# First attention batch: squares, narrowing steps and one subtraction in other places of the order, and unread products ahead of some waits

## The chip, the cores and the metric

One core of a Trainium2 chip. The metric is the device time of one execution in microseconds (us); several executions are run and the median is given. The engines are TensorE (PE; its weight loads are a row of their own, PEld), VectorE (DVE), ScalarE (ACT), GpSimd (POOL) and SyncE (SP), which only issues DMAs here.

## The reference

Three stages, all in float32. Attention over 4 batches, 12 heads, 448 positions and 64 channels, with q and k normalized by their root mean square:

```
q_n, k_n = rmsnorm(q, g_q), rmsnorm(k, g_k)        # x / sqrt(mean(x*x) + 1e-6) * g
scores = 1/sqrt(64) * q_n @ k_n.T ; scores -= max(scores, axis=-1)
attn = exp(scores) ; attn /= sum(attn, axis=-1) + 1e-9
x = attn @ v                                       # to [1792, 768]
h = x @ w_in ; g = h * clip(h + 3, 0, 6) / 6 ; x = g @ w_out      # 768 -> 2048 -> 768
```

Then a mixture of 8 experts with a fixed capacity of 224 tokens each: the gate's logits are sorted, every token gets an expert that still has room, and each expert applies a two-layer net with a relu. w_in and w_out arrive with 64 bits per element and have to be narrowed to float32 first.

## The kernel before, in words

**Units of work.** Attention runs over 24 pairs of heads, six to a batch: pair i is batch i // 6, and both heads of a pair are worked on together, one on partitions 0 to 63, one on 64 to 127. The dense layer 1 of a batch (`mlp1_atoms`, 16 units of 18 matmuls) can start when all six pairs of it are done, so the first batch of attention runs without it. From batch 1 on, matmuls of the dense layer of the batch before are dealt out between those of attention.

**What a pair does**, with the names that the prediction uses. `load` (L224): q and k by DMA. `squares` (L248, ScalarE, one call for q and one for k into two buffers `sq`), `fold` (L253, GpSimd, halves them), `sums` (L259, VectorE), `guess` (L269, VectorE), `invert` (L274: three Newton steps of four instructions each, on GpSimd for pairs 1 to 9, over one pair or a group of two), `norm` (L289, GpSimd: normalized `xn` of q and k). `transp` (L310) for q and k: four TensorE transposes each, then ScalarE writes the high part (`qh`, `kh`) and VectorE the low part (`ql`, `kl`). `s1` (L333), four chunks: two score matmuls and two row maxima `mx` on VectorE. `mt` (L345): the maxima transposed by TensorE, spread by VectorE (`mr`). `sT` (L353), four chunks: eight matmuls for the transposed scores with the maxima subtracted, two exponentials on ScalarE (`ph`). `pv` (L444): 16 matmuls for the output; ScalarE copies it to `xn_t`, of which there are two buffers. `psums` (L454): matmuls with ones sum the exponentials; ScalarE writes `rb`. From pair 6 on GpSimd first adds the exponentials in twos (`padd`, L439).

**The round trip.** The sums of a pair go to DRAM (`rs_out`, L469), come back in another layout (`rs_in`, L474), VectorE takes reciprocals (`rec`, L479), these go to DRAM (`r_out`, L485) and come back broadcast (`r_in`, L490). GpSimd multiplies `xn_t` with them (`xmul`, L495); `xsplit` (L499) writes the high part `xh` of the result on ScalarE and the low part `xl` on GpSimd. The `xl` of pair i frees the buffer into which `xn_t` of pair i+2 is copied. The last pair of batch 0 (pair 5) and of the whole run take another way (`av`, `normalize`, `xt`, L376 to L434).

**Narrowing.** `conv` (L150): for each of 16 units of w_in, a DMA of 768 KB, one ScalarE step and three VectorE steps (L141 to L144), and a DMA of the narrowed 384 KB. Two buffers hold the raw units, so the load of unit u+2 waits until the last step of unit u is done.

**The order.** Nothing is scheduled by a planner: every engine issues in program order, and that order is a list of events, each with a due time written by hand (`at`, L737, and the loop from L746). A pair takes 16 units of this time, pair i is shifted by 16 i, and the list is sorted. Within a pair `squares` come at -50, `invert` at -42 (groups of two from pair 4 to 9: -35.5), `transp` of q at -30 and of k at -28, `s1` from -24, `mt` at -9, `sT` from 0, `pv` at 15.6; in batch 0 (TX0, L79) the round trip and the two parts of x at 20, 23, 27, 29, 32.5, 39, 42 and 46. Unit u of w_in is loaded 14 ahead of 20 + 10 u (T_CI and D_CI, L81), its four steps stand at +0 to +3 and its store at +5 (L792 to L796). The squares of the second pair of a group stand 4 units after the first's (L752). Since every engine is strictly in order, an instruction that has to wait holds back all that stands behind it on its engine; so does a DMA in SP's queue that waits for its data.

PSUM tiles have eight buffers under one tag; a tile's first writer waits for the reader of the buffer's tenant before.

Of the kernel before, what the change touches and what calls it, by code (L numbers as in the profile page):

```python
# [10 lines left out]
BF16 = mybir.dt.bfloat16  # L11
# [10 lines left out]
def kernel(  # L22
# [14 lines left out]
    nc = tc.nc  # L37
# [8 lines left out]
    NP = H // 2  # L46
# [24 lines left out]
    T_SUMS, T_INV, T_INV0, NG0 = -50, -42, -35.5, 10  # L71
# [4 lines left out]
    T_ADD, T_PV, T_SUM = (6, 13), (15.6, 15.62, 15.64, 15.66), 15.7  # L76
    T_RS, T_RL, T_REC, T_RO, T_RB, T_X, T_XH, T_XL = 19.5, 21.5, 24, 25.5, 28, 33, 35.5, 39.5
    GD, WD2, C_ST = 12, 8, 5
    TX0 = (20, 23, 27, 29, 32.5, 39, 42, 46)  # L79
    QMAJOR = (NP - 1, B * NP - 1)  # L80
    T_CI, D_CI, T_CO, D_CO, T_CL = 20, 10, 180, 12, 14  # L81


    order = ExitStack()
# [3 lines left out]
    const = ctx.enter_context(tc.tile_pool(name="const", bufs=1, side="left"))  # L88
# [12 lines left out]
    def load_scales():  # L101
        for s in range(2):
            for t, src in ((gq8, g_q), (gk, g_k)):
                nc.sync.dma_start(t[64 * s:64 * s + 64, :], bass.AP(tensor=src.tensor, offset=src.offset, ap=[[1, D], [1, 1]]))
        nc.vector.tensor_scalar(gq8, gq8, 1.0 / math.sqrt(D), None, op0=OP.mult)

    half = const.tile([128, 1], F32, name="half")
    nc.vector.memset(half, 0.5)
# [201 lines left out]
    def transp(i, which):  # L310

        x = QKV[i][which]
        t = ps.tile([128, 512], F32, name="t", tag="b", bufs=8)
        for c in range(NCH):
            nc.tensor.transpose(t[:, c * CP:(c + 1) * CP], x[:, c].rearrange("p h d -> p (h d)"), ident[:CP, :CP])
        g = (gq8, gk)[which]
        h = apool.tile([128, S], F32R, name="qk"[which] + "h", bufs=OB)
        l = apool.tile([128, S], F32R, name="qk"[which] + "l", bufs=OB)
        if which == 0:
            order = "d (c p) -> d p c", "d (p c) -> d p c"  # L320
            tt, ho, lo = t[:, :S].rearrange(order[0], c=NCH), h.rearrange(order[1], c=NCH), l.rearrange(order[1], c=NCH)
        else:
            tt, ho, lo = t[:, :S], h, l
        hi = nc.scalar.activation(ho, tt, AF.Copy, scale=g)
        if which == 1:
            FIRST.setdefault("ka", hi)
        nc.vector.scalar_tensor_tensor(lo, tt, g, ho.bitcast(F32), op0=OP.mult, op1=OP.subtract)
        OPER.setdefault(i, []).extend((h, l))
# [4 lines left out]
    def s1(i, c):  # L333
        qh, ql, kh, kl = OPER[i]
        MX[i] = mxs[i % 2]
        pp = [ps.tile([128, 512], F32, name="s1", tag="b", bufs=8) for _ in ROWS]
        for s, r in enumerate(ROWS):
            mm = nc.tensor.matmul(pp[s][:CP, :S], qh[r, c * CP:(c + 1) * CP], kh[r], start=True, stop=True)  # L338
            MX.setdefault("first", mm)
        for s in range(2):  # L340
            mx = nc.vector.tensor_reduce(MX[i][:, s, c:c + 1], pp[s][:CP, :S], axis=AX.X, op=OP.max)  # L341
        if c == NCH - 1:
            FIRST.setdefault("mx", mx)

    def mt(i):  # L345
        t = ps.tile([128, 512], F32, name="t", tag="b", bufs=8)
        nc.tensor.transpose(t[:, :CP], MX[i].rearrange("p h c -> p (h c)"), ident[:CP, :CP])
        MR[i] = apool.tile([128, NCH, CP], F32R, name="mr")
        nc.vector.tensor_tensor(MR[i], t[:, None, :CP].to_broadcast([128, NCH, CP]), place, op=OP.mult)
# [103 lines left out]

    def psums(i):  # L454
        p = ps.tile([128, 512], F32, name="sm", tag="b", bufs=8)
        if i < NP:
            for c in range(NCH):
                for s in range(2):
                    r = (c % 2 * 2 + s) * QW
                    nc.tensor.matmul(p[r:r + QW, :S], ones32, PP[i, s, c][0], start=(c < 2), stop=(c >= 2))  # L460
        else:
            for n in range(2):
                for s in range(2):
                    r = (2 * n + s) * QW
                    nc.tensor.matmul(p[r:r + QW, :S], ones32, PA.pop((i, s, n)), start=True, stop=True)  # L465
        RB[i] = apool.tile([128, S], F32, name="rb", bufs=2)
        nc.scalar.activation(RB[i], p[:, :S], AF.Identity, bias=heps)
# [269 lines left out]
    def at(t, fn, *args):  # L737
        events.append((t, len(events), fn, args))
# [7 lines left out]
    for i in range(NH // 2):  # L746
        t = 16 * i
        at(t + T_LOAD, load, i)
        at(t + T_VLOAD, vload, i)
        g = GROUP[i]  # L750
        first = 16 * g[0]
        t_sq = first + T_SUMS + 4 * (i - g[0])  # L752
        at(t_sq, squares, i)
        if 2 <= i < NG0:
            at(t_sq + 2, fold, i)
            t_sq += 3
        at(t_sq, sums, i)
        late_g = 4 <= g[0] < NG0
        if i == g[-1]:
            at(t_sq if 2 <= i < NG0 else first + T_INV, guess, g)  # L760
            at(first + (T_INV0 if late_g else T_INV), invert, g)
# [28 lines left out]
    at(8 * H + 2, prefetch, 0)  # L790
    at(8 * H + 14, prefetch)
    for u in range(NF if wide else 0):  # L792
        for out_, t in ((0, T_CI + D_CI * u), (1, T_CO + D_CO * u)):
            at(t - T_CL, conv, (out_, u), -1)
            for part in (0, 1, 2, 3, C_ST):
                at(t + part, conv, (out_, u), part)  # L796
# [446 lines left out]
    for pi, (t, hfs) in enumerate(passes):  # L1243
        if t not in YT:
            YT[t] = gp.tile([128, DM], F32, name="ysb", bufs=2)
        pp = {hf: ps.tile([128, 512], F32, name="y", tag="b", bufs=8) for hf in hfs}
# [7 lines left out]
        for f in range(NF):  # L1254
            i, k = divmod(f, QF)
# [139 lines left out]
```

## Time and profile before

| | us |
|---|---|
| median of 3 runs | 1164.75 |
| lowest and highest | 1159.02, 1165.14 |
| the profiled execution, its own time | 1162.06 |
| its span, first to last instruction | 1160.2 |
| TensorE, weight loads, VectorE, ScalarE, GpSimd busy | 1099.2 (95%), 880.7 (76%), 692.2 (60%), 521.3 (45%), 464.6 (40%) |
| mean granted clock of TensorE | 0.979 of full speed |

The share of busy time is an average over stages: attention with the narrowing (to about 130 us for the first batch), attention with the dense layer between (to about 500), the dense layers, the routing and the experts. Busy time of TensorE is modelled from the starts of its matmuls and can't show how fast it ran; the granted clock and the distance between matmuls do. All times in rows are from the start of the span. In a timeline row the start comes first, then the busy time, and the brackets give how long the engine stood idle before and what released it.

### The profile page before, as it was taken

How to read it: one execution, taken by the hardware profiler on the slowest of the kernel's cores; microseconds unless marked ns; L12 is line 12 of the kernel's file. 1: busy time of each engine (PE TensorE's matmuls, PEld its weight loads, DVE VectorE, ACT ScalarE, POOL GpSimd, SP SyncE). 2: the span in 40 equal slices, each digit the busy share in tenths (PEclk: the TensorE clock that was granted, in tenths of full speed). 3: DMA queues.
4: the chain of work that ended last, by engine and by line, in shares of the span. 5: the costliest groups of instructions: out<-in, count | busy, mean ns of one | idle time of the engine just before them, and what ended most of it. 6: DMA issues, size and time to landing. Idle time of an engine off the chain costs nothing.

```text
span 1160.2 us, 19232 instructions
## 1 busy us (share of the span) xinstructions
PE 1099.2 (95%) x7073; PEld 880.7 (76%) x7073; DVE 692.2 (60%) x1440; ACT 521.3 (45%) x941; POOL 464.6 (40%) x410
## 2 busy tenths in 40 slices
PE   4978899999999999999999999999997999999997
PEld 3446556766766667787767888888887899999997
DVE  7877877886677845212341666666665846555550
ACT  4655555745545556533542111111114766666551
POOL 4665555664445533112444000000004677775540
PEclk9987989999999999999999999999998999999999
DMA  4575998978777887659996222222237888877731
GB/s 133 145 197 148 248 300 252 309 238 297 251 250 253 257 288 239 222 190 276 356 310 204 78 69 82 64 76 71 70 104 185 245 262 247 248 227 217 226 130 39
DMA packets 215357, 232.17 MB, mean 200 GB/s; under 512 B 28296, under 2 KB 188384, under 8 KB 215264
## 3 DMA queue, kind: packets, MB, share of 16 engines
q1 hardware_dynamic: 211936, 219.94, 61.6%
q0 software_dynamic: 3328, 11.01, 3.1%
q8 instruction: 55, 0.90, 0.3%
q14 instruction: 38, 0.31, 0.1%
HBM read 179.82 MB, written 51.09 MB: 199 GB/s over the span
## 4 chain that ended last, share of the span: by engine, by line
PE 67%; DVE 10%; DMA 9%; issue 5%; POOL 4%; ACT 3%; SPq 1%; POOLq 0%; DVEq 0%; ACTq 0%
PE y L1195 19%; PE h L559 15%; PE y L1347 8%; PE h L1283 5%; PE st L360 4%; PE av L449 4%; PE h L1285 3%; DMA w_hl<-w 2%; DMA we_s<-in_moe_w_dram 2%; DVE mx L341 2%; PE rt L988 1%; PE lg L601 1%; PE sm L465 1%; DMA gr<-g_dr 1%; DVE cv L143 1%
## 5 line engine op out<-in xcount | busy, mean ns | idle before, releaser
L559 PE MATMUL h<-xh,w 128*128 128x448 f32 x768 | 239.9, 382 | 1.0 <-DVE mx L341 0.5
L559 PEld LDWEIGHTS h<-xh,w 128*128 128x128 f32 x768 | 143.3, 191 | 35.9 <-issue 22.1
L559 PE MATMUL h<-xl,w 128*128 128x448 f32 x384 | 145.7, 379 | 0.0
L341 DVE TENSOR_REDUCE mx<-s 112x1 f32<-112x448 f32 x192 | 105.9, 611 | 51.6 <-PE s L338 51.3
L1133 ACT ACTIVATE g2h<-gr 128x512 fp32r<-128x512 f32 x60 | 37.9, 631 | 206.1 <-PE y L1195 161.6
L1195 PE MATMUL y<-woh,g2l 128*128 128x512 f32 (+1 forms) x448 | 124.8, 344 | 1.0 <-POOL g2l L1098 1.0
L1195 PE MATMUL y<-woh,g2h 128*128 128x512 f32 (+1 forms) x448 | 125.3, 345 | 0.0
L1195 PE MATMUL y<-wol,g2h 128*128 128x512 f32 (+1 forms) x448 | 125.2, 344 | 0.0
L1098 POOL TENSOR_TENSOR g2l<-gr,g2h 128x512 fp32r<-128x512 f32 x14 | 19.0, 1361 | 240.6 <-DMA gr<-g_dr 209.0
L119 POOL TENSOR_TENSOR wel<-we_s,weh 128x768 fp32r<-128x768 f32 x48 | 96.3, 2010 | 45.4 <-ACT weh L118 37.0
L118 ACT ACTIVATE weh<-we_s 128x768 fp32r<-128x768 f32 x107 | 88.4, 841 | 57.9 <-DMA we_s<-in_moe_w_dram 39.3
L119 DVE TENSOR_TENSOR wel<-we_s,weh 128x768 fp32r<-128x768 f32 x59 | 78.3, 1334 | 60.3 <-ACT weh L118 53.6
L371 ACT ACTIVATE ph<-st 112x448 f32<-112x448 f32 x192 | 93.0, 545 | 40.8 <-PE st L360 39.7
L442 POOL TENSOR_TENSOR pa<-ph 112x448 f32<-112x448 f32 x68 | 85.6, 1279 | 44.2 <-ACT ph L371 44.2
L1283 PE MATMUL h<-xe,weh 128*128 128x448 f32 x318 | 100.4, 375 | 2.0 <-DVE xe L1234 2.0
L559 PEld LDWEIGHTS h<-xl,w 128*128 128x128 f32 x384 | 73.2, 191 | 11.9 <-issue 7.0
L1195 PEld LDWEIGHTS y<-woh,g2l 128*128 128x128 f32 x448 | 72.0, 189 | 10.7 <-POOL g2l L1098 1.3
L1195 PEld LDWEIGHTS y<-woh,g2h 128*128 128x128 f32 x448 | 71.9, 189 | 10.6 <-issue 1.5
L1195 PEld LDWEIGHTS y<-wol,g2h 128*128 128x128 f32 x448 | 71.9, 189 | 9.1 <-issue 0.7
L1285 PE MATMUL h<-xe,wel 128*128 128x224 f32 x318 | 76.6, 268 | 0.0
L562 ACT ACTIVATE r<-h,half 128x448 f32<-128x448 f32 x64 | 40.6, 634 | 77.7 <-PE h L559 67.3
L497 POOL TENSOR_TENSOR xn_t<-xn_t,rb 128x448 f32<-128x448 f32 x22 | 25.8, 1175 | 119.7 <-DMA rb<-rec_dr 119.7
(252 smaller groups left out, 2386.1 us busy)
## 6 DMA issues: line engine op xcount, KB each, us to landing
we_s<-in_moe_w_dram SPq DMA_DIRECT2D x128, 384.0 KB
w<-w_hl SPq DMA_DIRECT2D x32, 768.0 KB
gr<-g_dr SPq DMA_DIRECT2D x52, 256.0 KB
wraw<-in_moe_w_in_dram SPq DMA_DIRECT2D x16, 768.0 KB
win_v<-w SPq DMA_DIRECT2D x32, 384.0 KB
w_hl<-w SPq DMA_DIRECT2D x16, 768.0 KB
wraw<-in_moe_w_out_dram SPq DMA_DIRECT2D x16, 768.0 KB
g_dr<-g SPq DMA_DIRECT2D x48, 224.0 KB
```

The lines of the kernel that those rows point to most:

```text
L118: nc.scalar.activation(hi, raw, AF.Copy)
L119: eng.tensor_tensor(lo, raw, hi.bitcast(F32), op=OP.subtract)
L341: mx = nc.vector.tensor_reduce(MX[i][:, s, c:c + 1], pp[s][:CP, :S], axis=AX.X, op=OP.max)
L360: nc.tensor.matmul(pp[s][:CP, :S], a[r], b[r], start=(n == 0), stop=(n == len(todo) - 1))
L371: nc.scalar.activation(e, pp[s][:CP, :S], AF.Exp)
L442: nc.gpsimd.tensor_tensor(PA[i, s, n], PP[i, s, 2 * n][0], PP[i, s, 2 * n + 1][0], op=OP.add)
L449: nc.tensor.matmul(p[r, :S], vvs[i % 2][:, s, c, V0:V0 + 64], PP[i, s, c][0], start=(c == 0), stop=(c == NCH - 1))
L559: nc.tensor.matmul(p[:, :S], lhs[:, c], x[:, c], start=(n == 0), stop=(n == 3 * NC - 1))
L1195: nc.tensor.matmul(pp[hf][:, :COLS[hf].stop - COLS[hf].start], a[:, f % QF], w[:, COLS[hf]], start=(f == 0 and n == 0), stop=(f == NF - 1 ...
L1283: mm = [lambda: nc.tensor.matmul(p[:, :4 * CP], wh[:, fo], x.rearrange("d k t -> d (k t)"), start=(c == 0), stop=(c == NC - 1), skip_group ...
L1285: lambda: nc.tensor.matmul(p[:, :2 * CP], wl[:, fo], x[:, 0], start=False, stop=False, skip_group_check=True)]
L1347: nc.tensor.matmul(p[:CP, :HW], a[:, f, tk], w[:, o], start=(f == 0 and n == 0), stop=(f == FB - 1 and n == 2))
```

## The change

Four things change. A tile `busy` of 128 x 512 ones in bf16 is written by GpSimd at the start, and a function `warm` issues matmuls of it into a PSUM tile that the next real matmul overwrites, so that nobody reads the products: 20 ahead of the first transposes, 3 ahead of the first `s1` chunk of pairs 1 to 7, 15 ahead of `mt` of pair 0 and 4 ahead of `mt` of pairs 1 to 7, 4 ahead of `psums` of pair 6: 88 in all. The low part of x of batch 0's pairs moves from 46 to 44.4, which puts it ahead of the Newton steps where those stand at 60.5 and 92.5 (pairs 1 and 3). The squares of pairs 5, 7 and 9 move from 4 to 6.1 behind those of pairs 4, 6 and 8, and their fold, sums and guess with them. The steps, loads and stores of units 0, 3, 5, 6, 8, 11, 13 and 14 of w_in move by +4.3, +6.3, +2.3, -1.7, +4.3, +6.3, +2.3 and -1.7.

```diff
--- before.py
+++ after.py
@@ -76,9 +76,10 @@
     T_ADD, T_PV, T_SUM = (6, 13), (15.6, 15.62, 15.64, 15.66), 15.7
     T_RS, T_RL, T_REC, T_RO, T_RB, T_X, T_XH, T_XL = 19.5, 21.5, 24, 25.5, 28, 33, 35.5, 39.5
     GD, WD2, C_ST = 12, 8, 5
-    TX0 = (20, 23, 27, 29, 32.5, 39, 42, 46)
+    TX0 = (20, 23, 27, 29, 32.5, 39, 42, 44.4)
     QMAJOR = (NP - 1, B * NP - 1)
-    T_CI, D_CI, T_CO, D_CO, T_CL = 20, 10, 180, 12, 14
+    T_CO, D_CO, T_CL = 180, 12, 14
+    T_CI = (24.3, 30, 40, 56.3, 60, 72.3, 78.3, 90, 104.3, 110, 120, 136.3, 140, 152.3, 158.3, 170)
 
 
     order = ExitStack()
@@ -103,6 +104,13 @@
             for t, src in ((gq8, g_q), (gk, g_k)):
                 nc.sync.dma_start(t[64 * s:64 * s + 64, :], bass.AP(tensor=src.tensor, offset=src.offset, ap=[[1, D], [1, 1]]))
         nc.vector.tensor_scalar(gq8, gq8, 1.0 / math.sqrt(D), None, op0=OP.mult)
+
+    busy = const.tile([128, 512], BF16, name="busy")
+    nc.gpsimd.memset(busy, 1.0)
+
+    def warm(p, n):
+        for _ in range(n):
+            nc.tensor.matmul(p, busy[:, :128], busy, start=True, stop=True)
 
     half = const.tile([128, 1], F32, name="half")
     nc.vector.memset(half, 0.5)
@@ -311,6 +319,8 @@
 
         x = QKV[i][which]
         t = ps.tile([128, 512], F32, name="t", tag="b", bufs=8)
+        if i == 0 and which == 0:
+            warm(t, 20)
         for c in range(NCH):
             nc.tensor.transpose(t[:, c * CP:(c + 1) * CP], x[:, c].rearrange("p h d -> p (h d)"), ident[:CP, :CP])
         g = (gq8, gk)[which]
@@ -334,6 +344,8 @@
         qh, ql, kh, kl = OPER[i]
         MX[i] = mxs[i % 2]
         pp = [ps.tile([128, 512], F32, name="s1", tag="b", bufs=8) for _ in ROWS]
+        if c == 0 and 0 < i < 8:
+            warm(pp[0], 3)
         for s, r in enumerate(ROWS):
             mm = nc.tensor.matmul(pp[s][:CP, :S], qh[r, c * CP:(c + 1) * CP], kh[r], start=True, stop=True)
             MX.setdefault("first", mm)
@@ -344,6 +356,7 @@
 
     def mt(i):
         t = ps.tile([128, 512], F32, name="t", tag="b", bufs=8)
+        warm(t, 15 if i == 0 else 4 if i < 8 else 0)
         nc.tensor.transpose(t[:, :CP], MX[i].rearrange("p h c -> p (h c)"), ident[:CP, :CP])
         MR[i] = apool.tile([128, NCH, CP], F32R, name="mr")
         nc.vector.tensor_tensor(MR[i], t[:, None, :CP].to_broadcast([128, NCH, CP]), place, op=OP.mult)
@@ -453,6 +466,8 @@
 
     def psums(i):
         p = ps.tile([128, 512], F32, name="sm", tag="b", bufs=8)
+        if i == NP:
+            warm(p, 4)
         if i < NP:
             for c in range(NCH):
                 for s in range(2):
@@ -749,13 +764,13 @@
         at(t + T_VLOAD, vload, i)
         g = GROUP[i]
         first = 16 * g[0]
-        t_sq = first + T_SUMS + 4 * (i - g[0])
+        late_g = 4 <= g[0] < NG0
+        t_sq = first + T_SUMS + (6.1 if late_g else 4) * (i - g[0])
         at(t_sq, squares, i)
         if 2 <= i < NG0:
             at(t_sq + 2, fold, i)
             t_sq += 3
         at(t_sq, sums, i)
-        late_g = 4 <= g[0] < NG0
         if i == g[-1]:
             at(t_sq if 2 <= i < NG0 else first + T_INV, guess, g)
             at(first + (T_INV0 if late_g else T_INV), invert, g)
@@ -790,7 +805,7 @@
     at(8 * H + 2, prefetch, 0)
     at(8 * H + 14, prefetch)
     for u in range(NF if wide else 0):
-        for out_, t in ((0, T_CI + D_CI * u), (1, T_CO + D_CO * u)):
+        for out_, t in ((0, T_CI[u]), (1, T_CO + D_CO * u)):
             at(t - T_CL, conv, (out_, u), -1)
             for part in (0, 1, 2, 3, C_ST):
                 at(t + part, conv, (out_, u), part)
```

## Rows read from the trace of the kernel before

**Rows 1.** Windows of 100 us: busy time of each engine, granted clock, DMA share, GB/s.

```profile
0.00:100.00 100.00, 74.40 (x483) 40.42 (x483) 77.29 (x156) 59.38 (x111) 54.74 (x106) 0.95 0.57 157
...
200.00:300.00 100.00, 96.97 (x567) 68.97 (x566) 78.20 (x131) 56.43 (x101) 55.52 (x43) 0.98 0.84 279
```

**Rows 2.** Waits by line, 0 to 110 us: total us, times, longest.

```profile
POOL xn_t L497 <- DMA rb<-rec_dr: 12.2, 4, 5.5
...
ACT xn_t L452 <- POOL xl L505: 9.8, 2, 7.3
```

**Rows 3.** Windows of the early stretches; after POOL come granted clock, DMA share, GB/s.

```profile
10.00:22.00 12.00, 7.86 (x35) 5.33 (x37) 9.30 (x21) 3.57 (x6) 7.17 (x19) 1.00 0.35 102
...
66.20:73.20 7.00, 5.96 (x22) 2.89 (x24) 6.44 (x13) 4.71 (x9) 3.56 (x7) 0.53 0.73 191
83.80:87.00 3.20, 3.20 (x18) 1.91 (x18) 3.14 (x6) 3.12 (x7) 1.62 (x2) 0.50 0.79 242
104.50:117.60 13.10, 13.10 (x70) 12.06 (x69) 8.87 (x14) 3.88 (x7) 6.52 (x9) 0.50 0.49 123
128.00:131.80 3.80, 3.65 (x15) 1.87 (x16) 2.33 (x2) 0.81 (x2) 3.80 (x3) 0.55 1.14 341
```

**Rows 4.** TensorE's timeline, 18 to 54 us.

```profile
18.31 2.01 PE L315 MATMUL t<-ident,xn 112*128 112x112 f32 x8
...
21.51 0.57 PE L360 MATMUL st<-mr,minus 64*112 64x448 f32 x2
...
22.42 0.37 PE L360 MATMUL st<-ql,kh 64*112 64x448 f32 x2
...
53.84 3.23 PE L449 MATMUL av<-ph,vv 112*64 112x448 f32 x16
```

**Rows 5.** TensorE's timeline, 28 to 128 us: its waits, and one row of transposes.

```profile
28.57 0.66 PE L338 MATMUL s<-kh,qh 64*112 64x448 f32 x4 [0.63 <-ACT kh L324]
...
64.42 0.32 PE L347 MATMUL t<-ident,mx 112*128 112x112 f32 x1 [1.69 <-DVE mx L341]
...
67.23 0.71 PE L338 MATMUL s<-kh,qh 64*112 64x448 f32 x2 [1.50 <-ACT kh L324]
...
81.00 0.97 PE L338 MATMUL s<-kh,qh 64*112 64x448 f32 x2 [2.59 <-ACT xn_t L452]
82.05 1.01 PE L315 MATMUL t<-ident,xn 112*128 112x112 f32 x8
...
97.58 0.46 PE L338 MATMUL s<-kh,qh 64*112 64x448 f32 x2 [1.00 <-ACT kh L324]
...
100.17 0.46 PE L360 MATMUL st<-qh,kh 64*112 64x448 f32 x2 [0.75 <-DVE kl L327]
...
102.36 0.46 PE L360 MATMUL st<-mr,minus 64*112 64x448 f32 x2 [1.33 <-DVE mr L349]
...
127.08 2.79 PE L465 MATMUL sm<-pa,ones 112*32 112x448 f32 x4 [2.16 <-POOL pa L442]
```

**Rows 6.** GpSimd's timeline, 71 to 106 us.

```profile
71.67 0.23 POOL L279 TENSOR_TENSOR st<-st 112x32 f32<-112x32 f32 x1
...
77.25 1.04 POOL L298 TENSOR_TENSOR xn<-ld_q,st 112x512 f32<-112x512 f32 x1
...
79.25 1.13 POOL L505 TENSOR_TENSOR xl<-xn_t,xh 128x448 fp32r<-128x448 f32 x1
...
101.86 0.24 POOL L279 TENSOR_TENSOR st<-st 112x32 f32<-112x32 f32 x1 [0.33 <-DVE st L272]
...
105.72 1.04 POOL L298 TENSOR_TENSOR xn<-ld_q,st 112x512 f32<-112x512 f32 x1
```

**Rows 7.** SP's issues, then VectorE's timeline, 100 to 109 us.

```profile
100.03 0.49 SPq L159 DMA_DIRECT2D wraw<-in_moe_w_in_dram  x1
100.61 0.68 SPq L476 DMA_DIRECT2D rs<-sum_dr  x1
...
108.59 0.28 DVE L482 TENSOR_TENSOR rr<-rs 112x8 f32<-112x8 f32 x1 [4.16 <-DMA rs<-sum_dr]
```

## The prediction

> **What bounds the kernel now.** I read the table of windows first: per 100 us, how busy each engine is. From 200 us on TensorE has work 97% of the time; in the first 100 us it has 74%, VectorE 77% [rows 1]. So the first batch of attention, up to about 130 us, is the only long stretch with room, and all parts of the change act there. What is gained before TensorE becomes dense at 130 us moves the rest earlier; what is lost moves it later.
>
> Then the waits of that stretch. ScalarE stood 9.8 us, once 7.3, before it could write a pair's unnormalized output, because the GpSimd subtraction that frees the buffer was late; GpSimd itself stood 12.2 us for the reciprocals' broadcast, which comes by DMA [rows 2]. The second is a loop: sums to DRAM, back, reciprocals, to DRAM, back, all issued in order by SP; no edit shortens it.
>
> Third, the clock. The granted clock is near 0.5, the 1.2 GHz level, in four stretches of 7.0, 3.2, 13.1 and 3.8 us before 132 us [rows 3]. For 10 to 22 us the record says 1.00 [rows 3], yet eight transposes take 2.01 us at 18.31, and a pair of score matmuls goes from 0.57 to 0.37 us between 21.51 and 22.42 [rows 4]; the same eight transposes take 1.01 us later [rows 5]. I take 10 to 22 us as the lower level. The Trainium skill, "TensorE: Matmul & The Clock Gate", Part 1, says that the throttled state is the default and that recorded gate events can't be fully trusted. Here the durations agree with it and the record doesn't; by the record the first 20 products could gain nothing.
>
> Last, TensorE's own waits, which say where products would be hidden and which moves can pay [rows 5].
>
> **The change, part by part.**
>
> *Price of a product.* No bf16 product of 512 columns is in the trace. Nearest: 16 matmuls of 448 columns in 3.23 us at the higher level [rows 4], 0.20 us each; times 512/448 is 0.23 us, and twice that, 0.46, at the lower level. Ends: 0.12 (should bf16 stream at twice that rate) and 0.46. I take 0.23, since it is the nearest row.
>
> *Start.* The 20 products need only a memset of GpSimd, which has nothing urgent before 9 us; TensorE idles until 9.99. Even at 0.46 they last 9.2 us from about 1.7, so they delay the first transposes by 1 us at most; I take 0. If they lift the clock, the four transposes of the first k take 0.5 instead of 1.0 us (half of the 2.01 of rows 4, halved again): -0.5, and GpSimd's loop of Newton steps starts that much earlier. The 15 products ahead of the first `mt` lie in a wait of 3.4 us for the row maxima: 15 x 0.23 = 3.4, cost 0; at 0.46 they would stick out by 3.5 us, the upper end.
>
> *Pair 1.* `mt` gets 4 products and the next `s1` 3: 1.6 us. Before that `s1` TensorE waited only 0.63 us [rows 5], and the 16 output matmuls queue behind it, so +1.0. Start and pair 1 together: +0.5.
>
> *Pairs 2 and 3.* VectorE is full from 39 to 59 us with the same work in another order; 4 products of each pair fall into waits for the maxima, the rest before work that waits for VectorE anyway. 0; without that cover 0.7 us a pair.
>
> *Squares of pairs 5, 7, 9.* They move behind the k operand `kh` in ScalarE's queue; today they wait there for a sum to free their buffer. TensorE waited 1.50 us for `kh` at 67.23 and 1.00 us at 97.58 [rows 5]: both can go. Fold, sums and guess come some 2 us later in the order, but the Newton steps of these groups are placed later still; 0.
>
> *Narrowing steps.* Unit 6 and the others leave VectorE's queue ahead of maxima and of `kl` and `mr`; waits of 0.75 at 100.17 and 1.33 us at 102.36 [rows 5] can go. Their DMAs move in SP's queue too: the load of unit 2 now waits for the last step of unit 0 ahead of `r_out(0)`, about +0.4 us for the round trip of pair 0, hidden by slack of the same size before its subtraction. The load of unit 8 goes behind `rs_in(4)`.
>
> *Low part of x.* `xl(1)` and `xl(3)` go ahead of 12 Newton steps and a normalization. The 7.3 us wait goes, and TensorE's wait of 2.59 at 81.00 with it. What is late next? `norm(6)`: its Newton steps now start after `xh(1)` and `xl(1)`, 0.6 + 1.13 us later than 71.67 [rows 6]. Alone, 12 steps took 3.9 us (101.86 to 105.72), here 5.6 (71.67 to 77.25) because narrowing ran on VectorE meanwhile [rows 6]. With 3.9, normalized k is ready at 79.4; with 5.6 at 81.1. Today its transposes start at about 82.5, the second half of the eight at 82.05 [rows 5]. So -3.1 or -1.4; I take -3.1, as the narrowing of unit 3 is now later. The Trainium skill, "SBUF — State Buffer", Who interferes with whom, has VectorE and GpSimd lock each other out for whole instructions where both use that pair. The two durations agree, and by that rule any overlap with units 3 or 4 brings 5.6 back: the sum would lose 1.7 us.
>
> *Products in pairs 4 to 7.* They stand behind the transposes, so they can't fill the wait for `norm(6)`; all 7 of pair 5/6 come after it, +1.6. In pair 4 four hide in the 1.69 us before 64.42 [rows 5]. Net over pairs 3 to 6, against the +0.5 so far: -3.1 + 1.6 = -1.5 in all, a step of -2.0. The clock, kept up over 66.2 to 73.2, buys 3 us there that then only lengthen the wait for `norm(6)`.
>
> *Pair 7.* -1.00 - 0.75 - 1.33, and +1.2 for products that don't hide (three at 0.23, and about half of the four before `mt(6)`, where today's wait is short): -1.9.
>
> *Pair 8's operands.* `xl(3)` ahead of the Newton steps of pairs 8 and 9 makes `norm(8)` 1.4 us later; in return `rs(4)` may land sooner. It landed about 8 us after its issue at 100.61, behind a 768 KB load issued at 100.03, and VectorE stood 4.16 us for it [rows 7]. Between 0 and -4.2; against the +1.4 I enter 0.
>
> *Pair 6's sums.* Its second addition now follows `xl(4)`: +1.1. The wait of 2.16 us at 127.08 [rows 5] holds the 4 products (0.9). If the clock stays up, 3.65 us of work at half speed [rows 3] saves 1.8. Net -0.7.
>
> **Sum.** +0.5 - 2.0 - 1.9 - 0.7 = -4.1 us. The profiled execution took 1162.06 us (span 1160.2 plus 1.9 around it), so 1158.0; it lies 2.7 below the median of the runs, 1164.75. On the median: 1160.6.
>
> **Rivals.**
>
> *The clock holds and no new wait appears.* Then the halves of the low stretches 66.2 to 73.2, 83.8 to 87 and 128 to 131.8 [rows 3] come back on the path (3.0 + 1.6 + 1.8), with the waits of 1.50, 2.59, 1.00, 0.75 and 1.33, less some 4 us of products: about -10, 1155; with the DMA of rows 7, 1150. For it: each wait removed stood before work at the low level. Against: `norm(6)`.
>
> *The round trip binds.* The reciprocals' loop sets each pair, and TensorE's gain turns into longer waits for it: GpSimd already stands 12.2 us there [rows 2]. Gain 0 to 1: 1164.
>
> *The products are on the path: slower.* The place is pairs 4 to 7. If the clock is already low when they are issued (a wait for `norm` comes ahead of them, and they can't fill it), 28 products cost 28 x 0.46 = 12.9 us, pair 1 another 1.0, less 1.50 + 1.00 + 2.08 of waits and 1 from elsewhere: +8, 1173. It decides from the point where a pair's wait before `mt` is shorter than 4 products, 1.8 us at the low level; the wait at 64.42 is 1.69, at 82.9 there is none. Against: at the higher level the same products cost half.
>
> *The moves do nothing* (another wait stands behind each) is the round-trip case.
>
> **How the numbers follow.** My forecast has 0.34, the round trip 0.12, the clock that holds 0.36, the products on the path 0.13; 0.05 is left to slips of DMA timing either way. A measurement of this kernel can tell about 0.5% (5.8 us) from no change: its own runs span 1159.02 to 1165.14. Forecast and round trip lie inside: 0.46. Faster: 0.36 and a slip, 0.38. Slower: 0.16. The forecast's own range is 1156 to 1166 (Newton steps 1.7, DMA 4.2, products at 0.12 or 0.46). The range 1150 to 1169 takes in the clock that holds with the DMA term, and the products on the path in half of the pairs.
>
> **What would show it.** Right: transposes of about 1.0 us per eight from 10 us on; no ScalarE wait for `xl` above 3 us; `kh` waits at pairs 5 and 7 gone; TensorE instead waiting for `xn` of pair 6 near 75 to 80 us; the first dense matmuls of `h` about 4 us earlier than 133.9. Wrong: TensorE dense more than 8 us earlier with no wait for `norm(6)`; or output matmuls of pairs 3 to 5 later than today, with products at 0.4 us and more just ahead of them.

## The result, and the profile after

The changed kernel takes 1171.35 us (median of 5 runs, 1170.57 to 1173.57), the kernel before beside it 1161.68 (5 runs): ratio 1.0077, interval 1.0057 to 1.0096, **slower by about 9 us**. The prediction said 1160.6, and 1150 to 1169. The forecast stood on the three runs known then (1164.75); its change was -4.1 us, the measured one is about +9. The profiled execution took 1173.57 us (span 1171.8). Two executions in the experiments below, one of e5 and one of e8, took about 3.6 ms and are left out of the medians.

First the windows, which answer to [rows 1], and three short ones to set beside [rows 3]; the columns are theirs.

```profile
0.00:100.00 100.00, 87.66 (x554) 44.31 (x554) 78.23 (x155) 57.35 (x107) 55.99 (x106) 0.93 0.53 153
...
200.00:300.00 100.00, 92.38 (x533) 62.68 (x530) 76.67 (x126) 52.57 (x95) 53.74 (x41) 0.98 0.84 271
```

```profile
10.00:22.00 12.00, 10.98 (x57) 5.93 (x58) 9.33 (x21) 4.22 (x8) 7.30 (x20) 0.72 0.38 111
...
81.00:86.00 5.00, 4.98 (x19) 3.12 (x21) 1.99 (x3) 1.79 (x3) 3.85 (x4) 0.50 0.77 221
...
110.00:122.00 12.00, 9.41 (x48) 8.52 (x48) 3.34 (x7) 2.17 (x4) 9.08 (x15) 0.50 1.01 274
```

TensorE is busier in the first 100 us (88% against 74%), but 24.1 us of that are 80 of the 88 products, which nobody reads. The low level of the clock around 70 us is gone (1.00 from 66 to 73 us); two later ones are there still, near 81 to 86 us and around 110 to 122. From 200 to 300 us TensorE is less dense than before (92% against 97%). Now TensorE's waits by line, 0 to 140 us (total, times, longest), two of the kernel before and then three of the changed one.

```profile
PE t L347 <- DVE mx L341: 7.1, 5, 3.4
PE s L338 <- ACT kh L324: 4.6, 5, 1.5
```

```profile
PE t L325 <- POOL xn L306: 9.3, 4, 4.9
...
PE s L350 <- ACT kh L334: 0.7, 1, 0.7
PE s L350 <- ACT xn_t L465: 0.5, 1, 0.5
```

The waits that the change was to remove are gone: 4.6 us for `kh` have become 0.7, the wait of 2.59 us behind `xn_t` [rows 5] is 0.5, those of 0.75 and 1.33 us for `kl` and `mr` do not appear, and the 7.1 us for row maxima are filled with products. In their place stand 9.3 us for GpSimd's normalized `xn`. In the profile before, that wait does not appear in this stretch. The next paragraphs follow this wait through the profile; whether it is what costs the time is for the experiments to say (e3).

**Where it starts: pair 6.** GpSimd's timeline in the changed kernel, to be read against [rows 6], with VectorE's below.

```profile
71.02 1.35 POOL L512 TENSOR_TENSOR xn_t<-xn_t,rb 128x448 f32<-128x448 f32 x1 [4.11 <-DMA rb<-rec_dr]
73.06 1.41 POOL L520 TENSOR_TENSOR xl<-xn_t,xh 128x448 fp32r<-128x448 f32 x1 [0.69 <-ACT xh L522]
74.43 0.55 POOL L287 TENSOR_TENSOR st<-st 112x32 f32<-112x32 f32 x1
75.06 0.93 POOL L288 TENSOR_TENSOR st<-st,st 112x32 f32<-112x32 f32 x1
76.08 0.87 POOL L289 TENSOR_SCALAR st<-st 112x32 f32<-112x32 f32 x1
77.03 0.25 POOL L290 TENSOR_TENSOR st<-st,st 112x32 f32<-112x32 f32 x1
...
80.93 1.04 POOL L306 TENSOR_TENSOR xn<-ld_k,st 112x512 f32<-112x512 f32 x1
```

```profile
74.92 0.96 DVE L151 SCALAR_TENSOR_TENSOR cv<-wraw,cv 128x768 int32<-128x768 int32 x1
75.91 0.96 DVE L152 SCALAR_TENSOR_TENSOR cv<-wraw,cv 128x768 int32<-128x768 int32 x1
```

The low part now runs at 73.06 us, before the Newton steps, as intended. The twelve steps take 5.4 us (74.43 to 79.85) and not 3.9, because two of VectorE's narrowing steps run beside them; a step of 0.25 us takes 0.87 to 0.93 there and 0.25 again as soon as VectorE is done at 76.87. The Trainium skill, "SBUF — State Buffer", Who interferes with whom, says that a VectorE instruction with two SBUF inputs contends with a GpSimd instruction that reads SBUF. The trace agrees: the long steps lie beside the two rows of VectorE, which have two inputs each. Normalized k of pair 6 is ready at 82.0 us; before, it was 79.3. TensorE's timeline:

```profile
81.02 2.01 PE L325 MATMUL t<-ident,xn 112*128 112x112 f32 x8 [4.95 <-POOL xn L306]
82.82 1.91 PE L113 MATMUL t<-busy 128*128 128x512 bf16 x4
84.53 0.39 PE L360 MATMUL t<-ident,mx 112*128 112x112 f32 x1
```

After 4.95 us of waiting the eight transposes take 2.01 us again, and the products 0.43 each, (84.53 - 82.82) / 4: the clock is at its lower level here, as the windows say. `mt(5)` starts 1.6 us later than before (82.90).

**How it grows: the reciprocals of pair 3.** VectorE, then SP, of the changed kernel.

```profile
87.77 2.21 DVE L353 TENSOR_REDUCE mx<-s 112x1 f32<-112x448 f32 x4 [2.19 <-PE s L350]
90.40 0.56 DVE L150 TENSOR_SCALAR cv<-cv 128x768 int32<-128x768 int32 x1 [0.41 <-ACT cv L149]
90.99 1.87 DVE L151 SCALAR_TENSOR_TENSOR cv<-wraw,cv 128x768 int32<-128x768 int32 x1
92.79 0.70 DVE L497 TENSOR_TENSOR rr<-rs 112x8 f32<-112x8 f32 x1
```

```profile
95.03 0.38 SPq L167 DMA_DIRECT2D wraw<-in_moe_w_in_dram  x1
95.47 0.53 SPq L502 DMA_DIRECT2D rec_dr<-rr  x1
```

In the kernel before, the three VectorE steps of unit 5 stood between the row maxima, filled the time in which VectorE now waits 2.19 us for scores, and were done when the sums came, at 89.97. Moved by +2.3, two of them (0.56 and 1.87 us) stand between the maxima and the reciprocals, and the third behind them; the load of unit 7, which needs the third, stands ahead of the reciprocals' store in SP's queue. So the reciprocals come 2.8 us later, their store 4.3 (91.14 before), and GpSimd's multiplication of pair 3 3.6 (103.97 against 100.39).

**What it hits: pair 8.** GpSimd's next stretch and TensorE's, first in the kernel before, then in the changed one.

```profile
100.39 1.14 POOL L497 TENSOR_TENSOR xn_t<-xn_t,rb 128x448 f32<-128x448 f32 x1 [1.69 <-DMA rb<-rec_dr]
...
106.72 1.04 POOL L298 TENSOR_TENSOR xn<-ld_k,st 112x512 f32<-112x512 f32 x1
```

```profile
115.43 0.39 PE L347 MATMUL t<-ident,mx 112*128 112x112 f32 x1
```

```profile
103.97 1.15 POOL L512 TENSOR_TENSOR xn_t<-xn_t,rb 128x448 f32<-128x448 f32 x1 [2.73 <-DMA rb<-rec_dr]
105.81 1.13 POOL L520 TENSOR_TENSOR xl<-xn_t,xh 128x448 fp32r<-128x448 f32 x1 [0.69 <-ACT xh L522]
106.90 0.24 POOL L287 TENSOR_TENSOR st<-st 112x32 f32<-112x32 f32 x1
...
108.79 0.94 POOL L290 TENSOR_TENSOR st<-st,st 112x32 f32<-112x32 f32 x1
...
113.38 1.04 POOL L306 TENSOR_TENSOR xn<-ld_k,st 112x512 f32<-112x512 f32 x1
```

```profile
113.47 1.01 PE L325 MATMUL t<-ident,xn 112*128 112x112 f32 x4 [2.59 <-POOL xn L306]
...
120.84 1.91 PE L113 MATMUL t<-busy 128*128 128x512 bf16 x4
122.55 0.39 PE L360 MATMUL t<-ident,mx 112*128 112x112 f32 x1
...
139.46 0.45 PE L574 MATMUL h<-xh,w 128*128 128x448 f32 x1
```

Normalized k of pair 8 ends at 114.42 us against 107.76, **6.6 us later**: 3.6 for the multiplication, 1.5 for the low part and its wait for `xh` ahead of the Newton steps, 1.5 because these take 5.4 us beside narrowing where they took 3.9. `mt(7)` is 7.1 us later than before (115.43), 1.7 of them its four products at the lower level (120.84 to 122.55), and the first matmul of `h` 5.6 (133.87). That is half of the 11.6 us between the two spans. The rest shows later: `mt(12)` starts 10.8 us later (238.5 against 227.7), and around 215 us ScalarE waits for the store of a split weight tile before it can go on to exponentials, and TensorE 4.2 us for these.

```profile
217.53 0.84 ACT L126 ACTIVATE w<-win_v 128x768 fp32r<-128x768 f32 x1 [4.46 <-DMA w_hl<-w]
```

### The profile page after: what moved, and what is told of

Read it like the earlier page. It is cut to its first block, busy times and chain, and to the rows that moved or that the text cites. A ratio compares the mean times of both kernels' runs of the same rounds, so it can differ in the third digit from the quotient of the medians.

```text
span 1171.8 us, 19396 instructions
## 1 busy us (share of the span) xinstructions
PE 1113.5 (95%) x7161; PEld 884.3 (75%) x7161; DVE 693.5 (59%) x1440; ACT 520.6 (44%) x941; POOL 468.2 (40%) x411
## 4 chain that ended last, share of the span: by engine, by line
PE 69%; DMA 9%; DVE 7%; POOL 5%; issue 5%; ACT 3%; SPq 1%; POOLq 0%; DVEq 0%; ACTq 0%
PE y L1210 18%; PE h L574 16%; PE y L1362 8%; PE h L1298 5%; PE av L462 4%; PE st L373 4%; PE h L1300 3%; DMA we_s<-in_moe_w_dram 2%; DMA w_hl<-w 2%; PE sm L480 1%; PE lg L616 1%; POOL pa L455 1%; PE rt L1003 1%; DMA sum_dr<-rb 1%; PE s L350 1%
## 5 line engine op out<-in xcount | busy, mean ns | idle before, releaser
L574 PEld LDWEIGHTS h<-xl,w 128*128 128x128 f32 x384 | 73.4, 191 | 12.0 <-issue 7.0
```

What stands on the lines that cost most here:

```text
L574: nc.tensor.matmul(p[:, :S], lhs[:, c], x[:, c], start=(n == 0), stop=(n == 3 * NC - 1))
```

## The experiments

Eighteen kernels, each timed beside the kernel before, e1 to e8 in three rounds and the others in five. In the expectations, P says that the products cost what is lost, O the order (the low part ahead of the Newton steps, and the held round trip of pair 3), N the narrowing moves by themselves, J these only together with the low part; later letters are explained where they stand. Medians in us; behind the ratio to the kernel before its interval. The kernel before had medians of 1160.41 to 1161.46 beside these, so two kernels are compared by their ratios. Then the ends of normalized k of pair 6 (k6), of the multiplication of pair 3 (x3), of normalized k of pair 8 (k8), and the start of the first `h` matmul, each from one profiled execution. That execution is not always a typical one: e5's took 1172.81 us, e4's 1159.49. e5 and e9 to e11 are made from the changed kernel by taking the other parts back; the tile of ones is still written in them, 0.51 us of GpSimd at the start.

| kernel | median | ratio | k6 | x3 | k8 | h |
|---|---|---|---|---|---|---|
| before | 1161.68 | | 79.3 | 101.5 | 107.8 | 133.9 |
| changed | 1171.35 | 1.0077 (1.0057, 1.0096) | 82.0 | 105.1 | 114.4 | 139.5 |
| e1 no products | 1169.26 | 1.0065 (1.0040, 1.0091) | 82.5 | 103.7 | 113.0 | 138.9 |
| e2 low part back | 1170.31 | 1.0066 (1.0037, 1.0096) | 80.7 | 106.7 | 114.1 | 138.1 |
| e3 narrowing back | 1164.01 | 1.0016 (0.9994, 1.0038) | 83.7 | 104.4 | 113.7 | 135.1 |
| e4 products alone | 1163.20 | 1.0014 (0.9994, 1.0033) | 79.0 | 102.0 | 108.5 | 131.8 |
| e5 narrowing alone | 1167.30 | 1.0046 (1.0029, 1.0062) | 82.0 | 107.3 | 114.9 | 137.0 |
| e6 late units back | 1173.53 | 1.0096 (1.0065, 1.0126) | 82.1 | 104.7 | 114.0 | 138.5 |
| e7 unit 5 back | 1170.76 | 1.0082 (1.0054, 1.0110) | 82.1 | 102.9 | 112.2 | 139.6 |
| e8 load 7 behind | 1172.60 | 1.0087 (1.0054, 1.0121) | 82.1 | 102.9 | 112.1 | 137.7 |
| e9 squares alone | 1162.72 | 1.0021 (1.0005, 1.0037) | 79.4 | 102.9 | 108.8 | 132.2 |
| e10 units 0, 3 alone | 1163.28 | 1.0017 (0.9996, 1.0038) | 81.0 | 103.0 | 109.3 | 133.8 |
| e11 units 6, 8 alone | 1162.32 | 1.0008 (0.9989, 1.0027) | 78.9 | 101.1 | 109.0 | 130.7 |
| e12 low part, products | 1163.02 | 1.0016 (1.0002, 1.0029) | 80.9 | 101.3 | 109.0 | 133.2 |
| e13 Newton ahead | 1173.52 | 1.0125 (1.0103, 1.0146) | 76.2 | 110.2 | 109.1 | 140.5 |
| e14 before, Newton ahead | 1168.58 | 1.0068 (1.0051, 1.0085) | 75.8 | 108.6 | 107.5 | 135.8 |
| e15 units 0, 3, 6, 8 back | 1169.24 | 1.0079 (1.0057, 1.0100) | 82.9 | 106.0 | 113.6 | 137.2 |
| e16 before, Newton on VectorE | 1168.08 | 1.0049 (1.0032, 1.0066) | 78.6 | 101.6 | 114.8 | 135.7 |
| e17 Newton on VectorE | 1171.34 | 1.0073 (1.0056, 1.0090) | 79.2 | 103.6 | 111.8 | 137.0 |
| e18 e12, Newton on VectorE | 1166.33 | 1.0037 (1.0022, 1.0051) | 78.4 | 100.5 | 113.5 | 135.4 |

### Each part by itself

**e1**, the changed kernel without products:

```diff
-        for _ in range(n):
+        for _ in range(0):
```

> The changed kernel without its 88 products; all moves stay. Theory O (the order: the low part of x ahead of the Newton steps, and the round trip of pair 3 held back by a load in SP's queue, cost most): the loss stays, 1168 to 1172 us, since the waits for the normalized operands of pairs 6 and 8 stay, and the clock falls more often. Theory P (the products are on the path): most of the 9.7 us comes back, 1161 to 1165 us.

It wins back 0.12% of 0.77%, 1.4 us, less than the intervals can tell: P falls. The granted clock is 1.00 from 66 to 73 us here too, without any product, so the low stretch of [rows 3] goes by the moves alone; in e4 it goes by the products alone.

**e2**, the low part back at 46:

```diff
-    TX0 = (20, 23, 27, 29, 32.5, 39, 42, 44.4)
+    TX0 = (20, 23, 27, 29, 32.5, 39, 42, 46)
```

> The changed kernel with the low part of x behind the Newton steps again. Theory O: the waits of TensorE for the operands of pair 6 (4.95 us) and pair 8 (2.59 us) shrink, the late round trip of pair 3 stays: 1165 to 1169 us. Theory P: no gain, 1170 to 1174 us, because ScalarE's wait of 7.3 us for the low part comes back on top of the products.

No gain beyond the intervals; O's 1165 to 1169 is missed. k6 is 1.3 us earlier, but k8 stays at 114.1: the low part's place is a small part of it.

**e3**, all narrowing steps back, the other three parts left:

```diff
-    T_CI = (24.3, 30, 40, 56.3, 60, 72.3, 78.3, 90, 104.3, 110, 120, 136.3, 140, 152.3, 158.3, 170)
+    T_CI = tuple(20 + 10 * u for u in range(16))
```

> The changed kernel with all narrowing steps, loads and stores at 20 + 10 u again. Theory O: the reciprocals of pair 3 leave some 4 us earlier and with them the operands of pair 8, and the gap of 4.2 us near 215 us is gone if the moved units 11, 13 and 14 make it: 1162 to 1167 us. Theory P: 1169 to 1172 us.

Most of the loss is back, 0.6% of 0.8%. O's time came true, but not its way. The store of pair 3's reciprocals leaves at 94.70 us (95.47 in the changed kernel, 91.14 before), k8 ends at 113.7, and TensorE waits longer for `xn` than in the changed kernel (9.3 us):

```profile
PE t L325 <- POOL xn L306: 12.0, 7, 4.6
```

So the late chain from pair 6 to pair 8 is there, and most of the loss is not. That chain alone doesn't explain the 9 us. What else the moved steps bring isn't shown; in the profiles `mt(7)` is 5.7 us late in e3 and 7.1 in the changed kernel, but `h` 1.3 and 5.6.

**e4**, the products alone on the kernel before (e3 with the two edits of e2 and of the squares, 6.1 to 4, undone as well):

> The kernel before with the 88 products and nothing else. Theory O: products cost 1 to 4 us or give a little back by the clock, 1160 to 1165 us. Theory P: 1168 us or more, as slow as the whole change.

Their cost can't be told from nothing.

**e5**, the narrowing moves alone (e1 and e2 together, and squares at 4):

> The kernel before with the moved narrowing steps, loads and stores alone: low part of x and squares as before, no products. Theory N (the narrowing moves by themselves cost most of the 9.7 us): 1167 to 1171 us, with the reciprocals of pair 3 leaving later than 91.1 us. Theory J (they cost only together with the low part of x ahead of the Newton steps): 1160 to 1164 us.

5.3 us (0.46%) without any other part: N stands, J falls. With e3 this shows the narrowing moves as the part that costs most. Normalized k of pairs 6 and 8 is as late as in the changed kernel, though neither low part nor squares moved. GpSimd in this kernel:

```profile
72.71 0.56 POOL L287 TENSOR_TENSOR st<-st 112x32 f32<-112x32 f32 x1
...
79.61 0.25 POOL L290 TENSOR_TENSOR st<-st,st 112x32 f32<-112x32 f32 x1
```

The steps that took 5.6 us before [rows 6] take 7.2 (72.71 to 79.86). The low part stands behind them here, so ScalarE's copy of pair 3's output is later too, and TensorE waits 7.3 us for it instead of 2.59 [rows 5].

**e9**, the squares alone:

```diff
-        t_sq = first + T_SUMS + 4 * (i - g[0])
+        late_g = 4 <= g[0] < NG0
+        t_sq = first + T_SUMS + (6.1 if late_g else 4) * (i - g[0])
```

> The kernel before with one edit: squares, fold, sums and guess of pairs 5, 7 and 9 at 6.1 instead of 4 behind their partners. Theory S (the later squares make the Newton steps of the groups late): normalized k of pair 8 ends at 112 us or later instead of 107.8, mt of pair 7 starts after 119 instead of 115.4, and the time is 3 to 5 us above before, about 1165. Theory N (the narrowing moves by themselves cost what is lost, and the squares are free): normalized k of pair 8 within 2 us of 107.8 and the time within 2 us of before.

A small cost, 0.21%, but not by S: k8 is only 1 us later. How it costs is open. **e12**, low part and products together, without squares and narrowing moves:

> The changed kernel with the squares and the narrowing steps back in their old places, so that the products of ones and the earlier low part of x remain. If squares and narrowing carry the loss (S and N together): at most 1163, about the time before, and below it by up to 3 us if the earlier low part of pairs 1 and 3 gains what it was moved for (the copy of pair 3's output waits less than 1 us instead of 7.3). If the low part ahead of the Newton steps is itself what makes the normalization of pairs 6 and 8 late: 1166 or more, with normalized k of pair 6 at 81 or later.

The copy of pair 3's output starts at 73.44 us (80.41 before), so ScalarE's long wait is gone; k6 is 1.6 us later, `mt(5)` 0.6, and nothing is gained. Against e4 the low part adds 0.02%.

So the parts alone are 0.14% (products), 0.02% (low part, e12 less e4), 0.21% (squares) and 0.46% (narrowing), together 0.83%; measured together 0.77%. Within the intervals they add up, and the narrowing moves are more than half.

### Which units

**e6**, units 11, 13 and 14 back at 130, 150 and 160; **e7**, unit 5 back at 70; **e8**, the load of unit 7 alone 1.2 later in the order, behind the store of pair 3's reciprocals.

> The changed kernel with units 11, 13 and 14 at 130, 150 and 160 again; the moves within the first batch stay. If these late units cost the second half of the loss (the gap of TensorE near 215 us): 1165 to 1167 us. If the loss is made in the first batch (theory N in its early form): 1169 to 1172 us.

> The changed kernel with unit 5 alone at 70 again, so that its last step stands ahead of the reciprocals of pair 3 and the load of unit 7 no longer waits behind them. If that unit holds the round trip of pair 3: the reciprocals leave near 92 instead of 95.5 us and the median is 1166 to 1169 us. If it is the sum of many moves: 1170 to 1172 us.

> The changed kernel with one DMA moved: the load of unit 7 is issued behind the reciprocals of pair 3 instead of ahead of them; no step moves. If the hold in SP's queue is what costs: the reciprocals leave 1.7 us earlier (93.8 instead of 95.5) and 2 to 4 us come back, 1167 to 1169 us. If VectorE's order is what costs: no change, 1170 to 1172 us.

None brings time back. In e7 and e8 the store of the reciprocals left 2.2 to 2.5 us earlier (93.02 and 93.28 against 95.47) and x3 came 2.2 us earlier, but k8 only by as much: it stayed at 112, 4 us late. e6 takes the second step of the loss away in its profile (`mt(12)` is 5.5 us late and not 10.8), and yet it isn't faster. Of the way that the profile shows, the held queue is one link, and it alone is not worth a measurable time. The other halves: **e10** and **e11**, units 0 and 3, and 6 and 8, moved alone on the kernel before; **e15**, the changed kernel with these four units back.

> The kernel before with the narrowing of units 0 and 3 alone moved (+4.3 and +6.3). Theory F (the first moved units cost: the load of unit 2 holds SP ahead of the sums of pair 0, and unit 3 stands beside the Newton steps of pairs 6 and 7): most of the 5 to 6 us of all narrowing moves, so 1166 or more, and normalized k of pair 6 at 81.5 or later against 79.3. Theory L (the units of pairs 5 to 7 cost, where the reciprocals of pair 3 and the Newton steps of pairs 8 and 9 are): within 2 us of before.

> The kernel before with the narrowing of units 6 and 8 alone moved (-1.7 and +4.3). Theory L (these stand next to the reciprocals of pair 3 and beside the Newton steps of pairs 8 and 9): 4 us or more above before, normalized k of pair 8 at 111 or later against 107.8. Theory F (units 0 and 3): within 2 us of before.

> The changed kernel with the narrowing of units 0, 3, 6 and 8 back in their old places; units 5, 11, 13 and 14 stay moved. If the early units carry the cost (2.2 us for 0 and 3, 1.3 for 6 and 8 when each pair of units was moved alone): 1166 to 1168. If the cost of the narrowing moves comes from unit 5 and the late ones together: 1170 or more. If it comes from the early units and grows when the squares are late as well: 1164, as with all units back.

F and L both miss: neither half is told from nothing. Putting both back wins nothing (0.79% against 0.77%), although putting all eight back wins 0.6% (e3). The cost isn't in one unit, and it doesn't add up unit by unit; how it is shared out stays open. Units 5, 11, 13 and 14 together were not tried.

### By which way it reaches TensorE

**e13** puts GpSimd's Newton steps and first normalization ahead of the multiplication whose broadcast it waits for, in the changed kernel; **e14** does so in the kernel before (-41.4, no other edit).

```diff
-    T_SUMS, T_INV, T_INV0, NG0 = -50, -42, -35.5, 10
+    T_SUMS, T_INV, T_INV0, NG0 = -50, -42, -40.3, 10
...
-    TX0 = (20, 23, 27, 29, 32.5, 39, 42, 44.4)
+    TX0 = (20, 23, 27, 29, 32.5, 40, 42, 44.4)
```

> The changed kernel with one edit in GpSimd's order alone: the Newton steps and the first normalization of the groups of pairs 6 and 7 and of pairs 8 and 9 stand ahead of the multiplication of x (pairs 1 and 3), whose broadcast GpSimd waits for, instead of behind its low part. Theory G (the lost time reaches TensorE through GpSimd's queue: normalized k of pairs 6 and 8 stands behind the reciprocals' round trip, which every move makes a little later): normalized k of pair 6 ends near 74 instead of 82.0 and of pair 8 near 109 instead of 114.4, TensorE's waits for xn fall from 9.3 to under 4 us, and the time falls by 5 us or more, to 1166 or below. Theory R (the round trip of pair 3 itself sets what follows, by another way): normalization is early as above, but the time stays at 1169 or more, since the multiplications come 3 to 5 us later still.

> The kernel before with the same edit of GpSimd's order alone. Theory G: normalized k of pair 6 ends 2 us or more ahead of 79.3, but the multiplication of pair 1 ends some 4 us later than 71.7 and its low part no earlier than 78, so the copy of pair 3's output goes on to wait and the gain is 0 to 4 us: 1157 to 1161. Theory R: the later multiplication costs, 1163 or more.

G falls: in e13 normalization is early, 76.2 and 109.1 us, and the kernel is slower still. What is late instead, in e14: GpSimd, ScalarE, TensorE.

```profile
107.48 1.13 POOL L497 TENSOR_TENSOR xn_t<-xn_t,rb 128x448 f32<-128x448 f32 x1
```

```profile
108.64 0.58 ACT L507 ACTIVATE xh<-xn_t 128x448 fp32r<-128x448 f32 x1 [8.42 <-POOL xn_t L497]
...
109.91 1.82 ACT L371 ACTIVATE ph<-st 112x448 f32<-112x448 f32 x4
```

```profile
110.49 3.26 PE L400 MATMUL av<-vv,ph 112*112 112x66 f32 x16 [5.08 <-ACT ph L371]
```

ScalarE stands 8.42 us before the high part of pair 3, with pair 5's last exponentials queued behind it, and TensorE waits 5.08 us for those. With the multiplications later, 5.2 us for pair 1 and 7.1 for pair 3 (x3 108.6 against 101.5), e14 loses 0.68%, 8 us, though its first matmul of `h` is only 1.9 us late. So both ends of GpSimd's stretch are needed by the others, ScalarE the multiplication and TensorE the normalization.

**e16**, the Newton steps of the two groups on VectorE, in the kernel before; **e17** in the changed one; **e18** in e12.

```diff
-        if 0 < g[0] < NG0:
+        if 0 < g[0] < 6:
```

> The kernel before with one edit: the Newton steps of the groups of pairs 6 and 7 and of pairs 8 and 9 run on VectorE (nine small instructions each instead of twelve on GpSimd, at the same place of the order). Theory K (GpSimd's stretch behind each reciprocals' broadcast, multiplication, Newton steps, normalization and low part, is what both TensorE and ScalarE wait for, whichever of them stands first): normalized k of pair 6 ends at about 75 instead of 79.3 and of pair 8 near 104.5 instead of 107.8, the low parts too come 3 to 4 us earlier, and the time falls by 2 to 6 us, to 1155 to 1159. Theory V (VectorE, which paces maxima and reciprocals, is the engine that binds): 2 us more on VectorE per group make it slower, 1163 or more.

> The changed kernel with the same edit. Theory K: both GpSimd stretches shorten by the 5.4 us that the Newton steps take there, normalized k of pairs 6 and 8 come 4 to 6 us earlier, and most of the loss goes: 1160 to 1165. Theory V: 1171 or more.

> The changed kernel with squares and narrowing in their old places (the low part ahead and the products stay) and the Newton steps of the two groups on VectorE. Theory K: as the kernel before with that edit or 1 to 2 us better, 1154 to 1159, since no wait for a low part or a normalization is left at pairs 5 to 7. Theory V: 1163 or more.

K's sums were wrong for both pairs (78.6 us and not 75 for pair 6, 114.8 and not 104.5 for pair 8), and its time too. V's time came true, but the profile shows another way. VectorE in e16, then GpSimd and TensorE:

```profile
108.27 0.17 DVE L482 TENSOR_TENSOR rr<-rs 112x8 f32<-112x8 f32 x1 [3.79 <-DMA rs<-sum_dr]
...
110.03 0.18 DVE L285 SCALAR_TENSOR_TENSOR st<-st 112x32 f32<-112x32 f32 x1
...
111.83 0.19 DVE L287 SCALAR_TENSOR_TENSOR st<-st,st 112x32 f32<-112x32 f32 x1
```

```profile
113.75 1.04 POOL L298 TENSOR_TENSOR xn<-ld_k,st 112x512 f32<-112x512 f32 x1
```

```profile
113.84 1.01 PE L315 MATMUL t<-ident,xn 112*128 112x112 f32 x4 [4.70 <-POOL xn L298]
...
121.22 0.39 PE L347 MATMUL t<-ident,mx 112*128 112x112 f32 x1
```

The nine steps take 2.0 us, but in VectorE's queue they stand behind the reciprocals of pair 4, which wait for a DMA until 108.27, and behind two narrowing steps. That makes e16 the cleanest case of the study: k6 (0.7 us earlier), x3 and the reciprocals of pair 3 (89.99 us) are about where they were, only k8 is 7.0 us late, `mt(7)` is 5.8 us late, and the kernel loses 0.49%, 5.7 us. But the first matmul of `h` is only 1.8 us late; the rest of the loss comes behind it, by a way that isn't shown, and a share of V isn't ruled out. e18 points the same way: against e12 k8 is 4.5 us later, k6 2.5 earlier, and the loss 0.37% against 0.16%, with intervals that overlap.

Over all 20 kernels: where x3 ended by 103.0 and k8 by 109.3 us (before, e4, e9 to e12), the ratios are at most 1.0021; where either was later, 1.0016 to 1.0125. It is no exact law: e3 has k8 at 113.7 and 1.0016. The start of `h` divides them without exception: up to 135.1 us the ratios are at most 1.0021, from 135.4 on 1.0037 or more. No kernel beat the one before.

## Why the prediction was wrong

**The step that failed** is "Narrowing steps", entered as a gain of 0.75 + 1.33 us and the largest wrong term: the moves cost 5.3 us by themselves (0.46%, e5), and with them taken back the changed kernel is 0.16% above the one before, not told from nothing (e3). The two waits did go. What wasn't asked was what the moved steps then stand ahead of: the reciprocals of pair 3, 2.8 us late, and the Newton steps, 7.2 us in e5. A wait of one load for one step in SP's queue was worked out, but for unit 0 and pair 0 (0.4, hidden), not for unit 5 and pair 3. These two are what the profile shows; by which way the moves cost the time stays open, since in e3 the reciprocals are late as well.

**Pair 8's operands** failed too: `norm(8)` 1.4 us later, set against a sooner `rs(4)`, entered as 0. It came 6.6 us later. The 1.4 was right by itself (1.5); two other terms were not seen: the multiplication ahead of it late by 3.6, and the Newton steps slowed by narrowing from 3.9 to 5.4 us, which the prediction weighed for pair 6 and forgot for pair 8, although the free time of [rows 6] at 101.86 was in its hands. What a late `norm(8)` costs isn't fixed: 0.49% in e16 for 7.0 us, 0.16% in e3, interval to 0.38%, for 6.0.

**Low part**: wait and mechanism right, the 7.3 us stall is gone, and `norm(6)` is late next, as named. It was put at 79.4 or, beside narrowing, at 81.1 us, and came at 82.0. The slowing beside narrowing was rightly foreseen (5.4 us against 5.6) and the -3.1 was the wrong choice; the rest is that the Newton steps began at 74.43, 1.0 us later than the 73.4 of the sum. During the wait of 4.95 us for it the clock fell (0.75 over 78 to 81 us, 0.50 over 81 to 86), and the next products took 0.43 us. Alone the part is worth nothing (e12 against e4), the round-trip rival's answer.

**Squares**, entered as the removal of waits of 1.50 and 1.00 us: the waits went, and the move costs 0.21% (e9), by a way that isn't shown.

**Products**: the price of 0.23 us was right at the higher level. TensorE's start:

```profile
1.61 5.87 PE L113 MATMUL t<-busy 128*128 128x512 bf16 x20 [1.61 <-POOL busy L109]
...
13.88 5.47 PE L113 MATMUL t<-busy 128*128 128x512 bf16 x15
19.19 0.26 PE L360 MATMUL t<-ident,mx 112*128 112x112 f32 x1
19.29 0.93 PE L325 MATMUL t<-ident,xn 112*128 112x112 f32 x8
...
21.96 0.82 PE L113 MATMUL s<-busy 128*128 128x512 bf16 x3
22.71 0.46 PE L350 MATMUL s<-kh,qh 64*112 64x448 f32 x2
```

Three take 0.75 us (21.96 to 22.71), 0.25 each. The 15 ahead of the first `mt` took 5.31 us, 0.35 each, and it started 1.3 us later than before (17.87): between the value taken and the upper end. Eight transposes then take 0.93 us and not 2.01 [rows 4], so the reading of 10 to 22 us as the lower level was right. Ahead of `mt(5)` and `mt(7)` four products took 1.7 us each time, at the lower level, and not the 0.9 of the price taken.

**The rivals.** The slower one had the right sign and nearly the size (1173), but its mechanism, products on the path, is worth 1.4 to 1.6 us, not told from nothing (e1, e4). The clock that holds, given the highest chance (0.36), failed by its condition: the clock did not hold at 81 to 86 and 110 to 122 us, and a new wait appeared. In e4 the record has the higher level through most of the four stretches of [rows 3] (1.00, 0.80, 0.93 and 1.00, with 0.50 at 78 to 85 us), and e4 isn't faster than before. What happened is nearer to the round-trip rival, which allowed no loss, because it took the loop of pair 3 as it stood.

Of the signs of being right, those on single waits came: the wait for `xn` of pair 6 (76 to 81 us), the `kh` waits gone and, but for 0.1 us, ScalarE's wait for `xl` down to 3 (3.1). The one on the sum, `h` 4 us earlier, did not: it came 5.6 us later.

## What to carry to other kernels

Work that is moved out of the way of one stall can cost more at its new place than the stall did (here 5.3 us against 2.1): write down what each moved instruction, and each DMA that needs it, now stands ahead of, for every copy of the pattern and not just the first. On an engine that serves two others, find both deadlines of its tightest stretch (here a multiplication for ScalarE and a normalization for TensorE); an order that is early for one is late for the other. Waits that vanish from a profile are no gain until the next product of that chain is seen to come earlier, and a wait that appears is no loss until a kernel without it is seen to be faster (e3 has the longer waits for `xn` and hardly any loss).

## What the runs showed of the hardware

A GpSimd step of 112 x 32 elements, 0.22 to 0.25 us, took up to 1.08 us beside VectorE's narrowing (0.94 at 108.79 in the changed kernel, 1.08 at 74.36 in e5), and twelve of them 3.9 us beside row maxima (before, from 101.86), 5.4 in the changed kernel and 7.2 in e5. Nine such steps on VectorE took 2.0 us. The granted clock was recorded as 1.00 for 10 to 22 us in the kernel before, although eight transposes took 2.01 us there, and as 0.72 in the changed one, where eight took 0.93 at 19.29 us: over this stretch the record can't be used to compare two kernels, and the durations can.
